# A linear-attention block gated with a SwiGLU block: the last 96 rows of w2 as 32-row matmuls, one row group per token tile

## The chip, the cores and the metric

The kernel runs on one core of one Trainium2 chip. The metric is the device time of one execution in microseconds. A core has TensorE (PE; its weight loads are listed apart as PEld), VectorE (DVE), ScalarE (ACT), GpSimd (POOL) and SyncE (SP), which here issues nearly all DMAs. The engines run their own instruction streams and wait for one another by semaphores.

## The reference, cut to what matters

```python
def _A_ref(x, wqkv, wo):                  # x: 1 x 2048 x 512, 32 heads of 16
    qkv = x @ wqkv                        # split in q, k, v
    phi = lambda t: jnp.where(t > 0, t + 1, jnp.exp(t)) + 1e-6
    pq, pk = phi(q), phi(k)
    kv = jnp.einsum("bhsd,bhse->bhde", pk, v)
    z = jnp.einsum("bhsd->bhd", pk)
    num = jnp.einsum("bhqd,bhde->bhqe", pq, kv)
    den = jnp.einsum("bhqd,bhd->bhq", pq, z)[..., None] + 1e-6
    return (num / den) @ wo               # heads put side by side again

def _B_ref(x, w1, w3, w2):                # F = 1376
    h = silu(x @ w1) * (x @ w3)           # 2048 x 1376
    return h @ w2                         # 2048 x 512

g = sigmoid((x * gate_w).sum(-1, keepdims=True))
return g * a + (1 - g) * b                # a = _A_ref(x, ..), b = _B_ref(x, ..)
```

All inputs and the output are bf16.

## The kernel before

The 2048 tokens are 16 tiles of 128 (NT), in 4 blocks of 512 (NTB blocks, TPB = 4 tiles each). F = 1376 is ten column groups of 128 (FC = 10) and a remainder of 96 (FR = 96), which starts at column F0 = 1280. A model dimension of 512 is four chunks of 128 (KC).

The order of work on each engine is the order in which the program issues it; nothing reorders it (the schedule is written out by hand). It has these stages.

First, for each token tile, the projections of q and k (line 169), their phi (lines 182 to 187), the running sum of pk over the tokens on POOL (line 201) and the accumulated product of pk and x (line 217). All weights and the transposed copies of x are loaded meanwhile, all on SP's queue; w2 comes last (lines 144 and 145). When the sum of pk is complete, SP transposes it (line 379), and a short chain of DVE work and two DMAs makes zb, the sum spread over all partitions.

Then come the four token blocks (line 463). In a block, `glu_step` runs for each of the ten column groups: four matmuls for the gate (line 264), four for the up projection (line 270), Silu on ACT (line 275) and the product on DVE (line 276), which writes the group's part of hT, the hidden layer with features on the partitions. In block 0 other work is set between the column groups: `kv_step` after group 2, `m2_step`, `z_order` and the first `den_products` after group 4, `den_step` after groups 5, 6, 8 and 9, and `rem_step(0)` after group 7.

`rem_step` computes the 96 remainder columns the other way round, with tokens on the partitions (16 matmuls of 193 columns, line 231: gate, up and the gating column), multiplies them on DVE into `hrem` (line 241), whose rows are padded with zeros to 128, and has a DMA transpose it into the eleventh chunk of hT (line 254).

`den_step(t)` makes the denominators of token tile t (DVE lines 287 to 294, POOL lines 283 and 298) and a DMA transposes the scaled tile into pqT (line 303).

After the column groups, `out_step` runs for each of the block's four token tiles. It sums a from pqT and M2 in four matmuls (line 429), which ACT scales by g into `aga` (line 434). Then it sums b in eleven matmuls (line 442): ten with 128 rows of hT and w2, the last one with the 96 remainder rows. DVE adds both (line 446), and SP stores the tile (line 459). Between the tiles of blocks 0 to 2 stand the `den_step` of the next block's tiles and, after tile 1, the `rem_step` of the next block. The last token tile of all is done in three column pieces.

PSUM has eight banks. `mm_tile` hands out banks 4 to 7 in turn, for column groups and remainder steps; `ab_tile` hands out banks 0 to 3 in turn, for the sums of a and b and for `kv_step` and `m2_step`. A matmul that takes a bank again waits until its last reader is done.

Of the kernel before, what the change touches and what calls it, by code (L numbers as in the profile page):

```python
# [9 lines left out]
ALU = mybir.AluOpType  # L10
AX = mybir.AxisListType
FP32 = mybir.dt.float32
BF16 = mybir.dt.bfloat16
# [3 lines left out]
def kernel(  # L17
# [17 lines left out]
    nc = tc.nc  # L35
    P = nc.NUM_PARTITIONS

    Bb, S, D = A_x.shape
    F = B_w1.shape[1]
# [5 lines left out]
    NTB = S // TB  # L45
    TPB = TB // P
    FC = F // P
    FR = F - FC * P
    F0 = FC * P
    HPC = P // Dh  # L50
    ZP = 4
    NR = 2 * FR + 1

    x2d = A_x.flatten_outer_dims()
    out2d = out.flatten_outer_dims()
# [5 lines left out]
    consts = ctx.enter_context(tc.tile_pool(name="consts", bufs=1))  # L61
# [13 lines left out]
        out=bmask[:], in_=bmask[:], pattern=[[-Dh, HPC], [0, Dh]], compare_op=ALU.is_ge,  # L75
# [3 lines left out]
        out=bmask[:], in_=bmask[:], pattern=[[Dh, HPC], [0, Dh]], compare_op=ALU.is_ge,  # L79
        fill=0.0, base=Dh - 1, channel_multiplier=-1,  # L80
    )
    hrem = [consts.tile([P, TPB, P], BF16, name=f"hrem{i}") for i in range(2)]
    for h in hrem:
        nc.gpsimd.memset(h[:], 0.0)
    zacc = consts.tile([P, D], FP32, name="zacc")
    zaccb = consts.tile([P, D], BF16, name="zaccb")
    zb = consts.tile([P, D], BF16, name="zb")
# [21 lines left out]
    dq = nc.sync  # L109
# [22 lines left out]
    with nc.allow_non_contiguous_dma(reason="gate column"):  # L132
        dq.dma_start(
            out=wr[:, :, 2 * FR : NR], in_=gate_w.rearrange("(kc d o) -> d kc o", d=P, o=1)
        )
# [7 lines left out]
    w2_r = B_w2[0:F0, :].rearrange("(fc f) d -> f fc d", f=P)  # L143
    dq.dma_start(out=w2[:, 0:FC, :], in_=w2_r)
    dq.dma_start(out=w2[:FR, FC, :], in_=B_w2[F0:F, :])

    pq = consts.tile([P, NT, D], BF16, name="pq")
    pqT = consts.tile([P, KC, S], BF16, name="pqT")
# [7 lines left out]
    bank = [psum.tile([P, D], FP32, name=f"bank{i}") for i in range(8)]  # L156
    turn = {"mm": 0, "ab": 0}

    def mm_tile():
        turn["mm"] += 1  # L160
        return bank[4 + (turn["mm"] - 1) % 4]

    def ab_tile():
        turn["ab"] += 1
        return bank[(turn["ab"] - 1) % 4]
# [56 lines left out]

    def rem_step(tb):

        hr = hrem[tb % 2]
        for half in range(2):
            ps = mm_tile()[:].rearrange("p (j n) -> p j n", j=2)
            for j in range(2):
                t = tb * TPB + half * 2 + j
                for kc in range(KC):  # L230
                    nc.tensor.matmul(  # L231
                        ps[:, j, 0:NR], lhsT=xT[:, kc, t * P : (t + 1) * P],
                        rhs=wr[:, kc, 0:NR], start=(kc == 0), stop=(kc == KC - 1),
                    )
            t0 = tb * TPB + half * 2
            sg = work.tile([P, 2, FR], BF16, tag="sgr", name="sgr")
            nc.scalar.activation(out=sg[:], in_=ps[:, :, 0:FR], func=ACT.Silu)
            nc.scalar.activation(
                out=th_all[:, t0 : t0 + 2], in_=ps[:, :, 2 * FR], func=ACT.Tanh, scale=0.5
            )  # L240
            nc.vector.tensor_tensor(
                out=hr[:, half * 2 : half * 2 + 2, 0:FR], in0=ps[:, :, FR : 2 * FR],
                in1=sg[:], op=ALU.mult,
            )
        tl = slice(tb * TPB, (tb + 1) * TPB)
        nc.vector.tensor_scalar(
            out=g_all[:, tl], in0=th_all[:, tl], scalar1=0.5, scalar2=0.5,
            op0=ALU.mult, op1=ALU.add,
        )
        nc.vector.tensor_scalar(  # L250
            out=omg_all[:, tl], in0=th_all[:, tl], scalar1=-0.5, scalar2=0.5,
            op0=ALU.mult, op1=ALU.add,
        )
        dq.dma_start(
            out=hT[tb][:, FC, :].rearrange("p (tt q) -> p tt q", q=P),
            in_=hr[:].rearrange("p tt f -> p (tt f)"), transpose=True,
        )

    def glu_step(tb, fc):
        fs = slice(fc * P, (fc + 1) * P)  # L260
        tok = slice(tb * TB, (tb + 1) * TB)
        g_ps = mm_tile()
        for kc in range(KC):
            nc.tensor.matmul(  # L264
                g_ps[:], lhsT=w1[:, kc, fs], rhs=xT[:, kc, tok],
                start=(kc == 0), stop=(kc == KC - 1),
            )
        u_ps = mm_tile()
        for kc in range(KC):
            nc.tensor.matmul(  # L270
                u_ps[:], lhsT=w3[:, kc, fs], rhs=xT[:, kc, tok],
                start=(kc == 0), stop=(kc == KC - 1),
            )
        sg = work.tile([P, TB], BF16, tag="sg", bufs=3, name="sg")
        nc.scalar.activation(out=sg[:], in_=g_ps[:], func=ACT.Silu)  # L275
        nc.vector.tensor_tensor(out=hT[tb][:, fc, :], in0=u_ps[:], in1=sg[:], op=ALU.mult)  # L276
# [28 lines left out]
    def den_step(t):  # L305

        den_sums(t)
        if t + 1 < NT:
            den_products(t + 1)
        den_scale(t)  # L310


    hT = {}
# [85 lines left out]
    def kv_step():  # L399
        kv_ps = ab_tile()[:].rearrange("p (c q) -> p c q", q=P)  # L400
        for c in range(KC):
            cs = slice(c * P, (c + 1) * P)
            for kc in range(KC):
                nc.tensor.matmul(  # L404
                    kv_ps[:, c, :], lhsT=wv[:, kc, cs], rhs=Gsb[:, kc, cs],
                    start=(kc == 0), stop=(kc == KC - 1),
                )
        nc.vector.tensor_tensor(
            out=kvT[:], in0=kv_ps,
            in1=bmask[:].rearrange("p h d -> p (h d)")[:, None, :].to_broadcast([P, KC, P]),  # L410
            op=ALU.mult,
        )

    def m2_step():
        for c in range(KC):
            ps = ab_tile()
            nc.tensor.matmul(ps[:], lhsT=kvT[:, c, :], rhs=wo[:, c, :], start=True, stop=True)  # L417
            if c % 2 == 0:
                nc.scalar.activation(out=M2[:, c, :], in_=ps[:], func=ACT.Copy)
            else:  # L420
                nc.vector.tensor_copy(out=M2[:, c, :], in_=ps[:])

    def out_step(tb, tt):
        t = tb * TPB + tt
        ts = slice(t * P, (t + 1) * P)
        tl = slice(tt * P, (tt + 1) * P)
        a_ps = ab_tile()
        for c in range(KC):
            nc.tensor.matmul(  # L429
                a_ps[:], lhsT=pqT[:, c, ts], rhs=M2[:, c, :],  # L430
                start=(c == 0), stop=(c == KC - 1),
            )
        aga = work.tile([P, D], FP32, tag="aga", name="aga")
        nc.scalar.activation(out=aga[:], in_=a_ps[:], func=ACT.Copy, scale=g_all[:, t : t + 1])  # L434
        o = work.tile([P, D], BF16, tag="o", bufs=3, name="o")
        last = t == NT - 1
        for lo, w in ((0, 2 * P), (2 * P, P), (3 * P, P)) if last else ((0, D),):
            cs = slice(lo, lo + w)
            b_ps = ab_tile()
            for fc in range(FC + 1):  # L440
                n = P if fc < FC else FR
                nc.tensor.matmul(  # L442
                    b_ps[:, 0:w], lhsT=hT[tb][:n, fc, tl], rhs=w2[:n, fc, cs],
                    start=(fc == 0), stop=(fc == FC),
                )
            nc.vector.scalar_tensor_tensor(  # L446
                out=o[:, cs], in0=b_ps[:, 0:w], scalar=omg_all[:, t : t + 1], in1=aga[:, cs],
                op0=ALU.mult, op1=ALU.add,
            )
            if t < 2:  # L450
                rows = out2d[0 : 2 * P, :].rearrange("(p j) d -> p j d", j=2)[:, t, :]
            else:
                rows = out2d[ts, :]
            if last and w == P:

                if lo + w < D:
                    continue
                cs = slice(2 * P, D)
            dq.dma_start(out=rows[:, cs], in_=o[:, cs])
# [3 lines left out]
    for tb in range(NTB):  # L463
        for fc in range(FC):
            glu_step(tb, fc)
            if tb == 0:
                if fc in den_at:
                    den_step(den_at[fc])
                if fc == 2:
                    kv_step()  # L470
                if fc == 4:
                    m2_step()
                    z_order()
                    den_products(0)
                if fc == 7:
                    rem_step(0)
        for tt in range(TPB):
            out_step(tb, tt)
            if tb + 1 < NTB:
                if tt == 0:  # L480
                    hT[tb + 1] = work.tile([P, FC + 1, TB], BF16, tag="hT", name="hT")
                if tt == 1:
                    rem_step(tb + 1)
                den_step((tb + 1) * TPB + tt)
# [30 lines left out]
```

## Time and profile before

| what | value |
|---|---|
| median of 3 runs | 179.36 us (178.71 to 179.49) |
| span of the profiled execution | 177.9 us, 2504 instructions |
| time of the profiled execution outside the span | the profile gives none; the median lies 1.46 us above the span |
| granted TensorE clock | 1.000 |
| PE busy | 174.3 us (98%), 879 instructions |
| PEld busy | 84.1 us (47%) |
| DVE busy | 101.5 us (57%) |
| ACT busy | 62.2 us (35%) |
| POOL busy | 63.5 us (36%) |
| DMA | 15.41 MB, mean 87 GB/s |

The span runs from the first to the last instruction of one execution; the time of a run is longer than that. Busy is the time in which an engine had an instruction under way. Matmuls overlap one another in the records, so 40 matmuls of 379 ns each need not take 40 x 379 ns; the spacing of their starts says what they cost. PEld, the weight loads, lie beside the matmuls.

### The profile page before, as it was taken

Reading aid. Unit: us, or ns where it says so; the run is one execution under the profiler, and the core shown is the slowest. Engines: PE = TensorE matmul, PEld = TensorE weight load, DVE = VectorE, ACT = ScalarE, POOL = GpSimd, SP = SyncE. Lnnn points to the kernel's source line nnn. Section 1 sums busy time; section 2 is a strip of 40 time slices with the busy share of each in tenths; the row PEclk is TensorE's granted clock in tenths of the full one; section 3 lists DMA queues with packets and bytes.
Section 4 is the critical chain, followed back from the end, with each engine's and each line's share of the span. In section 5 each row is a group of like instructions: output and inputs, shape, how many; then the busy total and the mean of one; then the engine's idle time right before and its main releaser. Section 6 shows DMA issues by size and latency. Waiting matters only on the chain.

```text
span 177.9 us, 2504 instructions
## 1 busy us (share of the span) xinstructions
PE 174.3 (98%) x879; PEld 84.1 (47%) x879; DVE 101.5 (57%) x195; ACT 62.2 (35%) x113; POOL 63.5 (36%) x105
## 2 busy tenths in 40 slices
PE   8999999999999999999999999999999999999993
PEld 5444444444454464644444464444445444444453
DVE  0299798888865888666344166634325564333222
ACT  3255444544744332331333223242321223342130
POOL 5077667557301676846300044540004432000000
DMA  6978959993103025243100013520000342000001
GB/s 175 266 209 233 168 100 315 391 350 111 33 0 29 0 55 66 66 95 106 29 0 4 0 33 85 94 57 4 0 0 29 88 92 59 0 0 0 29 33 59
DMA packets 29724, 15.41 MB, mean 87 GB/s; under 512 B 21552, under 2 KB 28048, under 8 KB 29712
## 3 DMA queue, kind: packets, MB, share of 16 engines
q1 hardware_dynamic: 29440, 15.25, 35.2%
q8 instruction: 7, 0.11, 0.3%
q10 hardware_dynamic: 272, 0.01, 0.1%
q14 instruction: 5, 0.04, 0.1%
HBM read 8.56 MB, written 2.10 MB: 60 GB/s over the span
## 4 chain that ended last, share of the span: by engine, by line
PE 98%; DVE 0%; issue 0%
PE bank L442 21%; PE bank L264 19%; PE bank L270 19%; PE bank L169 16%; PE bank L429 8%; PE bank L217 8%; PE bank L231 3%; PE bank L317 2%; PE bank L323 1%; PE bank L404 1%; PE bank L417 0%; DVE o L446 0%
## 5 line engine op out<-in xcount | busy, mean ns | idle before, releaser
L276 DVE TENSOR_TENSOR hT<-bank,sg 128x512 bf16<-128x512 f32 x40 | 27.3, 682 | 32.4 <-PE bank L270 32.4
L264 PE MATMUL bank<-xT,w 128*128 128x512 bf16 x160 | 41.1, 379 | 0.0
L270 PE MATMUL bank<-xT,w 128*128 128x512 bf16 x160 | 41.1, 379 | 0.0
L442 PE MATMUL bank<-w,hT 128*128 128x512 bf16 (+3 forms) x198 | 40.7, 355 | 0.0
L275 ACT ACTIVATE sg<-bank 128x512 bf16<-128x512 f32 x40 | 23.9, 597 | 46.7 <-PE bank L264 46.7
L298 POOL TENSOR_TENSOR pqs<-pq,rden 128x512 bf16<-128x512 bf16 x16 | 16.9, 1056 | 55.7 <-issue 48.2
L169 PE MATMUL bank<-wqk,xT 128*128 128x512 bf16 x128 | 31.2, 386 | 0.0
L442 PEld LDWEIGHTS <-hT 128*128 128x128 bf16 (+1 forms) x198 | 18.5, 98 | 19.8
L446 DVE SCALAR_TENSOR_TENSOR o<-bank,omg_all,aga 128x512 bf16<-128x512 f32 (+2 forms) x18 | 12.4, 692 | 25.6 <-PE bank L442 25.5
L201 POOL TENSOR_TENSOR zacc<-zacc,pk 128x128 f32<-128x128 f32 x56 | 23.3, 446 | 10.4 <-DVE pk L187 10.4
L270 PEld LDWEIGHTS <-w 128*128 128x128 bf16 x160 | 15.7, 98 | 18.9
L264 PEld LDWEIGHTS <-w 128*128 128x128 bf16 x160 | 15.6, 98 | 18.4
L434 ACT ACTIVATE aga<-bank,g_all 128x512 f32<-128x512 f32 x16 | 11.0, 688 | 28.9 <-PE bank L429 28.9
L169 PEld LDWEIGHTS <-xT 128*128 128x128 bf16 x128 | 12.6, 99 | 15.1 <-issue 0.6
L283 POOL TENSOR_TENSOR pr<-pq,zb 128x512 f32<-128x512 bf16 x16 | 18.5, 1156 | 0.1
L217 PE MATMUL bank<-pk,xN 128*128 128x512 bf16 x64 | 16.4, 379 | 0.0
L429 PE MATMUL bank<-M,pqT 128*128 128x512 bf16 x64 | 16.4, 378 | 0.0
L182 ACT ACTIVATE eq<-bank 128x512 bf16<-128x512 f32 x16 | 9.4, 598 | 16.0 <-PE bank L169 16.0
L187 DVE SCALAR_TENSOR_TENSOR pk<-bank,emk 128x512 bf16<-128x512 f32 x16 | 11.1, 692 | 1.6
L182 ACT ACTIVATE ek<-bank 128x512 bf16<-128x512 f32 x16 | 9.5, 597 | 7.1 <-PE bank L169 7.1
L187 DVE SCALAR_TENSOR_TENSOR pq<-bank,emq 128x512 bf16<-128x512 f32 x16 | 11.1, 692 | 0.5
L287 DVE TENSOR_REDUCE den<-pr 128x32 f32<-128x512 f32 x16 | 10.8, 676 | 0.0
(48 smaller groups left out, 82.6 us busy)
## 6 DMA issues: line engine op xcount, KB each, us to landing
w<-in_B_w_dram SPq DMA_DIRECT2D x3, 1280.0 KB, 10.1
out_dram<-o SPq DMA_DIRECT2D x15, 128.0 KB, 1.9
wqk<-in_A_wqkv_dram SPq DMA_DIRECT2D x4, 256.0 KB, 3.9
xN<-in_A_x_dram SPq DMA_DIRECT2D x1, 1024.0 KB, 5.8
xN<-in_A_x_dram SPq DMA_DIRECT2D x2, 256.0 KB, 3.1
xN<-in_A_x_dram SPq DMA_DIRECT2D x1, 512.0 KB, 3.7
wv<-in_A_wqkv_dram SPq DMA_DIRECT2D x1, 512.0 KB, 11.0
wo<-in_A_wo_dram SPq DMA_DIRECT2D x1, 512.0 KB, 12.0
```

The costliest lines, as they stand in the source:

```text
L169: nc.tensor.matmul(ps[:], lhsT=xT[:, kc, t * P : (t + 1) * P], rhs=w[:, kc, :], start=(kc == 0), stop=(kc == KC - 1),)
L182: nc.scalar.activation(out=e[:], in_=ps[:], func=ACT.Exp)
L187: nc.vector.scalar_tensor_tensor(out=dst, in0=ps[:], scalar=0.0, in1=em[:], op0=ALU.max, op1=ALU.add)
L201: nc.gpsimd.tensor_tensor(out=(zaccb if t == NT - 1 else zacc)[:, cs], in0=zacc[:, cs], in1=pk[t][:, cs], op=ALU.add,)
L217: nc.tensor.matmul(bank[kc][:], lhsT=xN[:, t, kc * P : (kc + 1) * P], rhs=pk[t][:], start=(t == 0), stop=(t == NT - 1),)
L264: nc.tensor.matmul(g_ps[:], lhsT=w1[:, kc, fs], rhs=xT[:, kc, tok], start=(kc == 0), stop=(kc == KC - 1),)
L270: nc.tensor.matmul(u_ps[:], lhsT=w3[:, kc, fs], rhs=xT[:, kc, tok], start=(kc == 0), stop=(kc == KC - 1),)
L275: nc.scalar.activation(out=sg[:], in_=g_ps[:], func=ACT.Silu)
L276: nc.vector.tensor_tensor(out=hT[tb][:, fc, :], in0=u_ps[:], in1=sg[:], op=ALU.mult)
L283: nc.gpsimd.tensor_tensor(out=pr[t][:], in0=pq[:, t, :], in1=zb[:], op=ALU.mult)
L429: nc.tensor.matmul(a_ps[:], lhsT=pqT[:, c, ts], rhs=M2[:, c, :], start=(c == 0), stop=(c == KC - 1),)
L442: nc.tensor.matmul(b_ps[:, 0:w], lhsT=hT[tb][:n, fc, tl], rhs=w2[:n, fc, cs], start=(fc == 0), stop=(fc == FC),)
```

## The change

For blocks 0 to 2 the 96 remainder rows of w2 are no longer the eleventh matmul of each token tile's sum. They are split into three sets of 32 rows (RG = 3, RP = 32). `rem_step` writes its products into `hrow` in an order in which, after one DMA transpose into `hrT`, partitions 32j to 32j + 31 of its piece r hold the features of set r for token tile j of the block. `w2x` holds the matching rows of w2 four times, once in each set of 32 partitions; four more DMAs load it behind w2. The new `rem_out_step` runs ahead of the block's `out_step`s: for each r it issues four 32-row matmuls, one for each token tile, which lie in four different row groups of the array and write four different banks. These begin the four sums of b, so banks 0 to 3 are held, one for each token tile, until the tile's ten 128-row matmuls have been added. The sums of a in these blocks take their banks from `mm_tile`. Block 3 keeps the form of before, with a single `hrem`. In block 0, `rem_step(0)` moves from after column group 7 to after column group 5.

```diff
--- before.py
+++ after.py
@@ -50,6 +50,8 @@
     HPC = P // Dh
     ZP = 4
     NR = 2 * FR + 1
+    RP = 32
+    RG = FR // RP
 
     x2d = A_x.flatten_outer_dims()
     out2d = out.flatten_outer_dims()
@@ -79,9 +81,11 @@
         out=bmask[:], in_=bmask[:], pattern=[[Dh, HPC], [0, Dh]], compare_op=ALU.is_ge,
         fill=0.0, base=Dh - 1, channel_multiplier=-1,
     )
-    hrem = [consts.tile([P, TPB, P], BF16, name=f"hrem{i}") for i in range(2)]
-    for h in hrem:
-        nc.gpsimd.memset(h[:], 0.0)
+    hrem = consts.tile([P, TPB, P], BF16, name="hrem")
+    nc.gpsimd.memset(hrem[:], 0.0)
+    hrow = [consts.tile([P, RG, TPB, RP], BF16, name=f"hrow{i}") for i in range(2)]
+    hrT = [consts.tile([P, RG, P], BF16, name=f"hrT{i}") for i in range(2)]
+    w2x = consts.tile([P, RG, D], BF16, name="w2x")
     zacc = consts.tile([P, D], FP32, name="zacc")
     zaccb = consts.tile([P, D], BF16, name="zaccb")
     zb = consts.tile([P, D], BF16, name="zb")
@@ -143,6 +147,9 @@
     w2_r = B_w2[0:F0, :].rearrange("(fc f) d -> f fc d", f=P)
     dq.dma_start(out=w2[:, 0:FC, :], in_=w2_r)
     dq.dma_start(out=w2[:FR, FC, :], in_=B_w2[F0:F, :])
+    w2x_r = B_w2[F0:F, :].rearrange("(r i) d -> i r d", i=RP)
+    for j in range(TPB):
+        dq.dma_start(out=w2x[j * RP : (j + 1) * RP, :, :], in_=w2x_r)
 
     pq = consts.tile([P, NT, D], BF16, name="pq")
     pqT = consts.tile([P, KC, S], BF16, name="pqT")
@@ -222,7 +229,7 @@
 
     def rem_step(tb):
 
-        hr = hrem[tb % 2]
+        tiled = tb + 1 < NTB
         for half in range(2):
             ps = mm_tile()[:].rearrange("p (j n) -> p j n", j=2)
             for j in range(2):
@@ -238,10 +245,18 @@
             nc.scalar.activation(
                 out=th_all[:, t0 : t0 + 2], in_=ps[:, :, 2 * FR], func=ACT.Tanh, scale=0.5
             )
-            nc.vector.tensor_tensor(
-                out=hr[:, half * 2 : half * 2 + 2, 0:FR], in0=ps[:, :, FR : 2 * FR],
-                in1=sg[:], op=ALU.mult,
-            )
+            up = ps[:, :, FR : 2 * FR]
+            if tiled:
+                for j in range(2):
+                    nc.vector.tensor_tensor(
+                        out=hrow[tb % 2][:, :, half * 2 + j, :],
+                        in0=up[:, j, :].rearrange("p (r i) -> p r i", i=RP),
+                        in1=sg[:, j, :].rearrange("p (r i) -> p r i", i=RP), op=ALU.mult,
+                    )
+            else:
+                nc.vector.tensor_tensor(
+                    out=hrem[:, half * 2 : half * 2 + 2, 0:FR], in0=up, in1=sg[:], op=ALU.mult,
+                )
         tl = slice(tb * TPB, (tb + 1) * TPB)
         nc.vector.tensor_scalar(
             out=g_all[:, tl], in0=th_all[:, tl], scalar1=0.5, scalar2=0.5,
@@ -251,10 +266,26 @@
             out=omg_all[:, tl], in0=th_all[:, tl], scalar1=-0.5, scalar2=0.5,
             op0=ALU.mult, op1=ALU.add,
         )
-        dq.dma_start(
-            out=hT[tb][:, FC, :].rearrange("p (tt q) -> p tt q", q=P),
-            in_=hr[:].rearrange("p tt f -> p (tt f)"), transpose=True,
-        )
+        if tiled:
+            dq.dma_start(
+                out=hrT[tb % 2][:], in_=hrow[tb % 2][:].rearrange("p r j i -> p (r j i)"),
+                transpose=True,
+            )
+        else:
+            dq.dma_start(
+                out=hT[tb][:, FC, :].rearrange("p (tt q) -> p tt q", q=P),
+                in_=hrem[:].rearrange("p tt f -> p (tt f)"), transpose=True,
+            )
+
+    def rem_out_step(tb):
+
+        for r in range(RG):
+            for j in range(TPB):
+                rows = slice(j * RP, (j + 1) * RP)
+                nc.tensor.matmul(
+                    bank[j][:], lhsT=hrT[tb % 2][rows, r, :], rhs=w2x[rows, r, :],
+                    start=(r == 0), stop=False,
+                )
 
     def glu_step(tb, fc):
         fs = slice(fc * P, (fc + 1) * P)
@@ -424,7 +455,8 @@
         t = tb * TPB + tt
         ts = slice(t * P, (t + 1) * P)
         tl = slice(tt * P, (tt + 1) * P)
-        a_ps = ab_tile()
+        tiled = tb + 1 < NTB
+        a_ps = mm_tile() if tiled else ab_tile()
         for c in range(KC):
             nc.tensor.matmul(
                 a_ps[:], lhsT=pqT[:, c, ts], rhs=M2[:, c, :],
@@ -436,12 +468,13 @@
         last = t == NT - 1
         for lo, w in ((0, 2 * P), (2 * P, P), (3 * P, P)) if last else ((0, D),):
             cs = slice(lo, lo + w)
-            b_ps = ab_tile()
-            for fc in range(FC + 1):
+            b_ps = bank[tt] if tiled else ab_tile()
+            nfc = FC if tiled else FC + 1
+            for fc in range(nfc):
                 n = P if fc < FC else FR
                 nc.tensor.matmul(
                     b_ps[:, 0:w], lhsT=hT[tb][:n, fc, tl], rhs=w2[:n, fc, cs],
-                    start=(fc == 0), stop=(fc == FC),
+                    start=(fc == 0 and not tiled), stop=(fc + 1 == nfc),
                 )
             nc.vector.scalar_tensor_tensor(
                 out=o[:, cs], in0=b_ps[:, 0:w], scalar=omg_all[:, t : t + 1], in1=aga[:, cs],
@@ -472,8 +505,10 @@
                     m2_step()
                     z_order()
                     den_products(0)
-                if fc == 7:
+                if fc == 5:
                     rem_step(0)
+        if tb + 1 < NTB:
+            rem_out_step(tb)
         for tt in range(TPB):
             out_step(tb, tt)
             if tb + 1 < NTB:
```

## The prediction

> **What bounds the kernel now.** I read the page's chain of the work that ended last first, then the groups of TensorE by form, then the same chain in order of time around the end of one token block, then the timeline of block 0 and the waits of the DMA-issuing SP.
>
> The chain by engine and line:
>
> ```profile
> PE 98%; DVE 0%; issue 0%
> PE bank L442 21%; PE bank L264 19%; PE bank L270 19%; PE bank L169 16%; PE bank L429 8%; PE bank L217 8%; PE bank L231 3%; PE bank L317 2%; PE bank L323 1%; PE bank L404 1%; PE bank L417 0%; DVE o L446 0%
> ```
>
> Nothing but TensorE sets the end, so a change is worth what it adds to or takes from TensorE's stream, and the waits that it puts into it. TensorE's waits have a single row, 0.8 us at the very start; there is no stall to recover.
>
> The forms of line 442, which the change touches (columns: line, engine, operation, out<-in, shapes, count | busy us, mean ns | idle before):
>
> ```profile
> L442 PE MATMUL bank<-w,hT 128*128 128x512 bf16 x150 | 34.8, 379 | 0.0
> L442 PE MATMUL bank<-w,hT 96*128 96x512 bf16 x15 | 5.7, 381 | 0.0
> L442 PEld LDWEIGHTS <-hT 96*128 96x128 bf16 x18 | 1.8, 98 | 1.8
> ```
>
> A 96-row matmul lasts as long as a 128-row one, so the last quarter of the array is paid for and unused. The 379 ns run from start to finish; the spacing comes from the chain in time (start, length, count):
>
> ```profile
> 68.27 2.38 PE bank L442 x11
> 70.64 0.87 PE bank L429 x4
> 71.51 2.38 PE bank L442 x11
> 73.89 1.34 PE bank L231 x16
> ```
>
> Eleven matmuls in 2.38 us are 216 ns each, the 96-row one among them; a matmul thus still runs 379 - 216 = 163 ns after the next has started. The weight loads (98 ns) lie wholly under the matmuls.
>
> The timeline where block 0 passes to its output, cut to what the steps below use:
>
> ```profile
> 52.06 1.06 PE L404 MATMUL bank<-Gsb,wv 128*128 128x128 bf16 x16
> ...
> 52.96 1.03 PE L264 MATMUL bank<-xT,w 128*128 128x512 bf16 x4
> ...
> 59.00 1.03 PE L264 MATMUL bank<-xT,w 128*128 128x512 bf16 x4
> 59.27 0.69 DVE L276 TENSOR_TENSOR hT<-bank,sg 128x512 bf16<-128x512 f32 x1 [0.70 <-PE bank L270]
> ...
> 62.32 3.86 SPq L303 DMA_TRANSPOSE pqT<-pqs  x2
> ...
> 64.29 0.61 DVE L241 TENSOR_TENSOR hrem<-bank,sgr 128x192 bf16<-128x192 f32 x2
> ...
> 66.27 1.22 SPq L254 DMA_TRANSPOSE hT<-hrem  x1
> ...
> 67.24 1.03 PE L429 MATMUL bank<-M,pqT 128*128 128x512 bf16 x4
> ```
>
> Line 404 is the useful neighbour: 16 matmuls with 16 different weight loads go by in 52.96 - 52.06 = 0.90 us, so a load-and-matmul pair can start every 56 ns. And SP:
>
> ```profile
> SPq L379 <- POOL zaccb L201: 9.8, 1, 9.8
> ```
>
> SP stands idle for 9.8 us between the last weight load and the transpose of zaccb.
>
> **TensorE, the part that decides.** Per block the change removes four 96-row matmuls: 4 x 216 = 864 ns. It adds twelve 32-row matmuls with twelve weight loads. No 32-row matmul stands in this trace, so the price is bounded.
>
> If four row groups stream side by side with no stagger, three rounds cost 3 x 216 = 648 ns, 216 ns less than before. If the pairs start 56 ns apart as at line 404, round follows round (4 x 56 = 224 ns, a hair over one matmul's 216), and the next full-height matmul must wait for the last group: 11 x 56 + 216 = 832 ns, 32 ns less than before. If the groups do not run side by side, twelve cost 12 x 216 = 2592 ns, 1728 ns more. I take 832, since line 404 is the nearest row with a new weight load for every short stretch of streaming.
>
> Twice per block the array also changes between full height and four groups. The trace has no such change. The lower bound is nothing: 128-row and 96-row matmuls follow each other at 216 ns today. The upper bound is that the array empties (163 ns, the overhang above) and the next weights are loaded only then (98 ns): 261 ns. I take the 163 ns, because loads run ahead everywhere in this trace: 326 ns per block.
>
> Per block: -864 + 832 + 326 = +294 ns; over three blocks +0.88 us. With bounds on both terms, groups side by side: from 3 x (648 - 864) = -0.65 us to 3 x (832 - 864 + 522) = +1.47 us.
>
> By the Trainium skill, "TensorEngine Tiling (Array Packing)", Key Properties, changing the tiling mode, not just the tile, drains TensorE; it gives no time, and no row here can show it. This is the rule that speaks against the change, and with the overhang as its price the sum is the +0.88 us above; without it, -0.1 us. By the skill's "TensorE: Matmul & The Clock Gate", Part 3, tiles of different row groups start about 4 ns apart, and four 32-row matmuls of 512 columns measured 3.07 times as fast as in sequence; with that stagger a round is 216 + 12 = 228 ns and the three blocks gain 3 x (864 - 684) = 0.54 us if the switches are free.
>
> **The rest, all beside the stream.**
>
> DVE: two 128x192 products per block (0.61 us, 305 ns each) become four 128x96. From 305 ns and the 682 ns of a 128x512 one, 1.18 ns per column and 78 ns fixed: 191 ns each, 766 against 610, +0.16 us per block. DVE waits for TensorE before 32 of the 40 products of line 276, 32.4 us in all or 1.0 us each, which covers it; uncovered it would be 0.5 us in all.
>
> rem_step(0) goes from after column group 7 to after 5. TensorE would run it from 59.00 to 60.34. DVE then does den_sums(0) (to 61.16), four products (61.93) and two small ones (62.26); the product of group 6 becomes ready at 59.27 + 1.34 + 1.73 = 62.34, so it is not late. Group 7 reuses the first remainder bank at about 62.07, freed at 61.55: 0.5 us in hand. On SP the remainder's transpose now stands ahead of pqT's tiles 1 to 3 and behind tile 0 (issued 62.32, 1.22 us): issued at 63.5, and with the page's 2.4 us to landing there at 65.9. The row-group matmuls want it at 67.24, 1.3 us later. At its old place it would land at 66.27 + 2.4 = 68.7, 1.4 us late. What is pushed back on SP is at most one issue, and pqT's tile 1, issued at about 65.2 to land at 67.6, is wanted only near 71.
>
> The transposes themselves shrink from four 128-column blocks to three. The four w2x loads (96 KB each, 0.39 MB, 1.1 us at the 350 GB/s of slice 9 of the page) go on SP between line 145 (its issue ends at 37.0) and line 379 (46.88): the 9.8 us idle covers them. Uncovered, zaccb's transpose would wait, and the z chain behind it has about 2.5 us (64.7 to 67.2) before pqT is wanted.
>
> Banks: a's four tiles move to the banks of the column groups; each reuses one given back by a product or Silu two tiles earlier. b's banks were read a whole block of column groups before, so holding them early waits for nobody. One memset fewer at the start is off the chain. All of this at nothing.
>
> **The sum.** The profiled span is 177.9 us; the page gives no time for that execution beyond its span, and the median of the shown runs is 179.36, 1.46 us more, which I leave as it is. 177.9 + 0.88 = 178.8 of span, 180.2 us by the median.
>
> **Rivals.**
>
> Free switches, the other side: groups stream together and loads stay ahead, as they do at 216 ns for 96 rows next to 128. Then only the rounds count: -0.1 to -0.65 us, 178.7 to 179.3, about 179.0. Against it: nothing in the trace shows a change of array layout. It decides when a switch costs under 16 ns at 56 ns spacing, or under 108 ns without stagger. The 4 ns rule above lands here, at 178.8.
>
> No overlap of groups: the change doesn't do what it says. 3 x 1.73 = +5.2 us, 184.5; with switches at 163 ns 185.5. For it: every matmul here costs 216 ns whatever its rows. Against: the groups share neither rows nor output banks.
>
> Loads set the pace: each group's load shows its whole 98 ns, 11 x 98 + 216 = 1294 ns, plus 326 for the switches, +0.76 us per block: +2.3 us, 181.6. Against it: line 404 at 56 ns. A late hrT in block 0, should SP run over 1.3 us behind, costs up to the 1.4 us of the old place and ends between 180.2 and 181.6 too.
>
> **Chances.** Groups side by side with switches paid (0 to +1.6 us): 0.43. Free switches: 0.28. Slow loads or a late transpose: 0.13. No overlap: 0.16. A difference of 0.5% (0.9 us) is about what a measurement of this kernel can tell from no change. The most that the sum allows is a gain of 0.65 us, so faster by over 0.5% needs runs that fall luckily on top of the free case: 0.08. My own case straddles the bound at +0.88: half of it, with slow loads and no overlap, makes slower by over 0.5%: 0.50. Within 0.5%: 0.42. The likeliest case's own range is 179.3 to 180.9. The range over cases runs from 178.6, the free case's end, to 182.0, past the slow loads, and leaves out no overlap.
>
> **What would show it.** In the changed profile the twelve 32-row matmuls of a block should take about 0.83 us from first start to last start plus 0.22, with starts 56 ns apart; a gap of about 160 ns should stand before the first of them and before the first matmul of line 429 behind them. No gap means free switches; starts 216 ns apart mean no overlap, starts 98 ns apart slow loads. A wait of TensorE on hrT in block 0 would break the SP step; a wait on a DVE row at line 276 the bank step. Any TensorE time changed outside these stretches would make the prediction wrong.

## The result and the profile after

The changed kernel took 179.63 us (median of 20 runs, 179.33 to 180.08), the kernel before 179.31 us beside it (20 runs, 178.58 to 179.80). The ratio is 1.0023, 95% interval 1.0012 to 1.0034: slower by 0.3 us, about a third of the 0.88 us that was forecast. Part of the spread is the clock: the five of the changed kernel's 20 runs with a granted clock of 0.997 or 0.998 took 179.87 to 180.08 us, the fifteen at 1.000 took 179.33 to 179.90. The profiled span of the changed kernel is 178.0 us, of the kernel before 177.9.

The chain that ended last, by engine and line, of the changed kernel:

```profile
PE 97%; issue 1%; ACT 0%; DVE 0%; ACTq 0%
PE bank L475 20%; PE bank L295 20%; PE bank L301 19%; PE bank L176 16%; PE bank L461 8%; PE bank L224 8%; PE bank L238 3%; PE bank L348 2%; PE bank L285 1%; PE bank L435 1%; PE bank L448 0%; PE bank L354 0%; ACT sg L306 0%; DVE o L479 0%; ACTq L306 0%
```

The lines are renumbered (264 is now 295, 270 is 301, 429 is 461, 442 is 475) and the row-group matmuls are line 285. TensorE still sets the end. Of the 903 matmul records 17 are missing from this trace; in the second profile of the same kernel (e9 below), which has all 903, "issue" is 0%.

The new group by its tile hrT (count: duration min/median/max in ns, first and last start in us):

```profile
L285 PEld LDWEIGHTS <-hrT x36: 90/93/94, 67.2 to 130.5; 32*128 32x128 bf16 x36
L285 PE MATMUL bank<-w2x,hrT x36: 374/374/385, 67.2 to 130.7; 32*128 32x512 bf16 x36
```

And TensorE's timeline of the changed kernel at the end of block 0 (start, us, instruction, count):

```profile
66.20 1.03 PE L301 MATMUL bank<-xT,w 128*128 128x512 bf16 x4
67.17 0.82 PE L285 MATMUL bank<-w2x,hrT 32*128 32x512 bf16 x12
67.92 1.04 PE L461 MATMUL bank<-M,pqT 128*128 128x512 bf16 x4
```

Twelve matmuls of 374 ns lie within 0.82 us, so they run side by side. Read record by record, the four of a round start within 10 ns of one another (67.165, 67.168, 67.171, 67.175) and the next rounds begin at 67.391 and 67.607. Two gaps frame them. The last full-height matmul starts at 66.853 and the first row-group one 312 ns later, 96 more than the usual 216. The last row-group matmul starts at 67.616 and the next full-height one 307 ns later, 91 more. The first weight load of the new kind does not run ahead either: it starts at 67.160, 5 ns before its matmul, where loads otherwise start some 200 ns before theirs.

The section on the kernel before says that nothing reorders the work of an engine. For weight loads the records show otherwise: the four loads of the second round start at 67.175 to 67.185, ahead of that round's first matmul at 67.391, although each belongs to its own matmul call. They go into the row groups in which the first round's matmuls have only just begun.

To see where the time of a run goes, I cut each execution in three: up to the first matmul of kv_step, from there to the last matmul's start, and from there to the end of the span. The middle piece as a window of the profile (start and end, length, then the busy time of PE, PEld, DVE, ACT and POOL), before and after:

```profile
52.06:174.91 122.85, 122.85 (x642) 60.22 (x641) 62.91 (x122) 37.33 (x71) 35.40 (x33) 1.00 0.18 39
```

```profile
51.89:174.69 122.80, 122.02 (x653) 59.50 (x665) 62.51 (x128) 37.33 (x71) 35.36 (x33) 1.00 0.16 38
```

Everything that the change does to TensorE's stream, with its rounds, switches, banks and the moved step, makes this piece 0.05 us shorter. (PE's 122.02 after is no idle time: 12 of the missing records lie here, 653 matmuls against 665 loads.) The end is another matter. From the last matmul's start to the end of the span it is 3.02 us before and 3.27 after. The program ends with SP waiting for the DMA semaphores, the counters by which a DMA reports that it has landed; the waits on the last store (us in total, times, longest), before and after:

```profile
SPq L510 <- DMA out_dram<-o: 0.9, 1, 0.9
```

```profile
SPq L545 <- DMA out_dram<-o: 1.2, 1, 1.2
```

The last store itself lands 1.53 us after its issue before and 1.54 after. The DMAs take eight semaphores in turn. With 72 DMAs the last store falls on the last of them, with 76 on the fourth. SP then checks the eight in five instructions, one every 62 to 69 ns; the last store's stands in the fifth of these before and in the first after, so four more checks (0.26 us) come behind the landing instead of ahead of it. Before, the first check ran at 175.9 us with the store still under way; after, at 176.9, once it had landed (first and last start stand behind the durations):

```profile
L510 SPq EVENT_SEMAPHORE  x7: 17/28/28, 175.9 to 177.9; - x7
```

```profile
L545 SPq EVENT_SEMAPHORE  x7: 17/28/28, 176.9 to 177.9; - x7
```

So the rows give -0.05 + 0.26 = +0.21 us, which is theory T of the expectations below: a ratio of 1.0012 against the measured 1.0023 (1.0012 to 1.0034).

### The profile page after: what moved, and what is told of

It is laid out like the page before. It is cut to its first block, busy times and chain, and to the rows that moved or that the text cites. A ratio compares the mean times of both kernels' runs of the same rounds, so it can differ in the third digit from the quotient of the medians.

```text
span 178.0 us, 2542 instructions
## 1 busy us (share of the span) xinstructions
PE 173.1 (97%) x886; PEld 83.4 (47%) x903; DVE 101.1 (57%) x201; ACT 62.2 (35%) x113; POOL 63.0 (35%) x104
## 4 chain that ended last, share of the span: by engine, by line
PE 97%; issue 1%; ACT 0%; DVE 0%; ACTq 0%
PE bank L475 20%; PE bank L295 20%; PE bank L301 19%; PE bank L176 16%; PE bank L461 8%; PE bank L224 8%; PE bank L238 3%; PE bank L348 2%; PE bank L285 1%; PE bank L435 1%; PE bank L448 0%; PE bank L354 0%; ACT sg L306 0%; DVE o L479 0%; ACTq L306 0%
## 5 line engine op out<-in xcount | busy, mean ns | idle before, releaser
L295 PE MATMUL bank<-xT,w 128*128 128x512 bf16 x157 | 40.9, 379 | 0.3
L301 PE MATMUL bank<-xT,w 128*128 128x512 bf16 x156 | 40.4, 379 | 0.1
L475 PE MATMUL bank<-w,hT 128*128 128x512 bf16 (+4 forms) x182 | 37.7, 353 | 0.2
L475 PEld LDWEIGHTS <-hT 128*128 128x128 bf16 (+1 forms) x186 | 17.4, 98 | 18.4
```

Source lines behind the costliest of these rows:

```text
L295: nc.tensor.matmul(g_ps[:], lhsT=w1[:, kc, fs], rhs=xT[:, kc, tok], start=(kc == 0), stop=(kc == KC - 1),)
L301: nc.tensor.matmul(u_ps[:], lhsT=w3[:, kc, fs], rhs=xT[:, kc, tok], start=(kc == 0), stop=(kc == KC - 1),)
L475: nc.tensor.matmul(b_ps[:, 0:w], lhsT=hT[tb][:n, fc, tl], rhs=w2[:n, fc, cs], start=(fc == 0 and not tiled), stop=(fc + 1 == nfc),)
```

## The experiments

Of each profile the three pieces are given in one table at the end of this section. They are cut from the records of the trace.

**e1, full height.** As the changed kernel, but four 96-row matmuls at the head of the block's sums; hrem and its transpose as before the change.

```diff
-        for r in range(RG):
-            for j in range(TPB):
-                rows = slice(j * RP, (j + 1) * RP)
-                nc.tensor.matmul(
-                    bank[j][:], lhsT=hrT[tb % 2][rows, r, :], rhs=w2x[rows, r, :],
-                    start=(r == 0), stop=False,
-                )
+        for j in range(TPB):
+            nc.tensor.matmul(
+                bank[j][:], lhsT=hT[tb][:FR, FC, j * P : (j + 1) * P], rhs=w2[:FR, FC, :],
+                start=True, stop=False,
+            )
```

> The changed kernel with everything moved and held as it is there, but the remainder of a block done in four 96-row full-height matmuls at the head of the sums instead of twelve 32-row ones; the four w2x loads are issued and not read. Theory T (the rounds run at 3 x 216 ns and two switches of about 100 ns each eat the gain, so TensorE's stream is the same as before to 0.05 us; the time that is left over comes from the end of the program, where SP waits for its eight DMA semaphores one after the other and the last store's semaphore now stands four places earlier, 4 x 65 ns = 0.26 us): about 0.26 us over the kernel before, like the changed kernel; four matmuls take 864 ns from the first start to the next matmul's start, with no gap. Rival S (the row groups or the switches cost the 0.3 us in a way that the trace does not show): the kernel before to within 0.1 us.

Measured: 179.44 us against 179.46, ratio 0.9998 (0.9984 to 1.0012). The middle piece is 122.81 us, the end 3.27 us, both as in the changed kernel (122.80 and 3.27). By its rows T is right: rounds with switches cost what four full-height matmuls cost. The time of the runs leaves both theories standing, since T's 1.0012 is the interval's upper end and S's 1.0 lies in the middle.

**e2, the loads alone.** The kernel before with the four w2x loads and nothing that reads them.

```diff
     dq.dma_start(out=w2[:FR, FC, :], in_=B_w2[F0:F, :])
+    w2x_r = B_w2[F0:F, :].rearrange("(r i) d -> i r d", i=32)
+    for j in range(TPB):
+        dq.dma_start(out=w2x[j * 32 : (j + 1) * 32, :, :], in_=w2x_r)
```

> The kernel before with nothing but the four w2x loads added behind w2; nothing reads them. Theory T: 76 DMAs instead of 72, the last store falls on the fourth of the eight semaphores, so SP has four more waits after it has landed: +0.26 us over the kernel before, and after the last store's landing about 1.1 us to the end of the span where before shows 0.85. Rival S: no change. Rival L (the loads delay the z chain or other transfers that TensorE waits for): a wait of TensorE on a DMA or a DVE row in block 0.

Measured: 179.70 us against 179.46, ratio 1.0013 (0.9999 to 1.0027). The middle piece is that of the kernel before, 122.85 us; the end is 3.28 us. From the landing of the last store to the end of the span it is 1.11 us, against 0.85 before, as foretold, and SP's last wait grew:

```profile
SPq L514 <- DMA out_dram<-o: 1.2, 1, 1.2
```

Four loads that no instruction reads lengthen the end by 0.26 us and leave TensorE's stream alone: against L.

**e3, eight loads.** The changed kernel with each load cut in two.

```diff
-        dq.dma_start(out=w2x[j * RP : (j + 1) * RP, :, :], in_=w2x_r)
+        for lo, hi in ((0, 1), (1, RG)):
+            dq.dma_start(out=w2x[j * RP : (j + 1) * RP, lo:hi, :], in_=w2x_r[:, lo:hi, :])
```

> The changed kernel with each w2x load cut in two, so eight loads and 80 DMAs; same bytes. Theory T: the last store is back on the last of the eight semaphores, 0.26 us less than the changed kernel: between 0.1 us under and 0.1 us over the kernel before. Rival S: like the changed kernel, 0.3 us over the kernel before. Rival L: a little more than the changed kernel, since SP issues four DMAs more.

Measured: 179.23 us against 179.46, ratio 0.9990 (0.9976 to 1.0004). With four DMAs more than the changed kernel, the end is back at 3.00 us and SP's wait at the value of before:

```profile
SPq L546 <- DMA out_dram<-o: 0.9, 1, 0.9
```

The count of DMAs, not their work, sets the end.

**e4, rounds set apart.** In blocks 1 and 2 one round ahead of column group 8, one ahead of group 9, one in the old place.

```diff
+            if tb in (1, 2) and fc >= FC - 2:
+                rem_out_step(tb, [fc - (FC - 2)])
             glu_step(tb, fc)
...
-            rem_out_step(tb)
+            rem_out_step(tb, range(RG) if tb == 0 else [2])
```

> The changed kernel, with the three rounds of blocks 1 and 2 set apart: one ahead of column group 8, one ahead of group 9, one where all three were. Eight switches more in all. Theory T with a fixed price of about 100 ns for each switch: +0.8 us over the changed kernel, 1.1 over the kernel before, and the same 0.1 us gap ahead of and behind each round. If the 0.1 us belongs to the first use of hrT and not to the switch: no change against the changed kernel. With the 163 ns of the prediction for each switch: +1.3 us over the changed kernel.

Measured: 180.54 us against 179.46, ratio 1.0054 (1.0038 to 1.0071). The middle piece is 123.67 us, 0.87 more than in the changed kernel: 109 ns for each of the eight switches. TensorE's timeline in block 1:

```profile
94.44 1.03 PE L301 MATMUL bank<-xT,w 128*128 128x512 bf16 x4
95.40 0.39 PE L285 MATMUL bank<-w2x,hrT 32*128 32x512 bf16 x4
95.73 1.04 PE L295 MATMUL bank<-xT,w 128*128 128x512 bf16 x4
```

Four full-height matmuls take 0.86 us; the round stands 0.96 behind their start, and the next full-height matmul starts 0.33 behind the start of the round instead of 0.216. The price is one of the switch and is paid in both directions.

**e5, six rounds.** Each round issued twice.

```diff
-        for r in range(RG):
+        for n in range(2 * RG):
+            r = n % RG
...
-                    start=(r == 0), stop=False,
+                    start=(n == 0), stop=False,
```

> The changed kernel with the three rounds issued twice in each stretch, which adds the remainder twice to b; the number of switches stays. Theory T: a round is one matmul's 216 ns and no more, so 3 blocks x 3 rounds x 216 = +1.94 us over the changed kernel, with the gaps ahead of and behind the stretch as they are. If the 0.2 us of a block's gaps grow with the number of 32-row matmuls (weight loads that show): +2.5 us. With starts 56 ns apart as in the prediction: 12 x 56 = 672 ns a block, +2.0 us, to be told from T by the starts in the trace.

Measured: 181.19 us against 179.41, ratio 1.0104 (1.0080 to 1.0128). The middle piece is 124.75 us, 1.95 more than in the changed kernel: nine more rounds at 216 ns. The stretch of block 0 in TensorE's timeline:

```profile
67.07 1.47 PE L286 MATMUL bank<-w2x,hrT 32*128 32x512 bf16 x24
68.48 1.04 PE L462 MATMUL bank<-M,pqT 128*128 128x512 bf16 x4
```

It lasts 1.41 us to the next matmul, against 0.75 for three rounds. Within a round the starts stand 2 to 5 ns apart and not 56, and the twenty-four weight loads cost nothing beyond the rounds.

**e6, one load.** The kernel before with the first of the four loads only.

```diff
     dq.dma_start(out=w2[:FR, FC, :], in_=B_w2[F0:F, :])
+    w2x_r = B_w2[F0:F, :].rearrange("(r i) d -> i r d", i=32)
+    dq.dma_start(out=w2x[0:32, :, :], in_=w2x_r)
```

> The kernel before with one more load (96 KB into a tile that nothing reads), so 73 DMAs. Theory T: the last store falls on the first of the eight semaphores and SP has seven waits more after its landing, 7 x 65 ns = 0.46 us over the kernel before: a quarter of the added bytes of the four loads, and a larger loss than theirs. Rival L (bytes or DMA issues cost): a quarter of the four loads' loss, under 0.1 us. TensorE's stretch from the first matmul of kv_step to its last matmul stays at 122.85 us in both.

Measured: 179.41 us against 179.41, ratio of the runs 1.0011 (0.9997 to 1.0024). The middle piece is 122.85 us, as expected; the end is 3.11 us, 0.09 more than before, not 0.46. The count of seven waits was wrong: SP checks the eight semaphores in five instructions, three of them two DMA semaphores at once, and the first semaphore shares the third. So two checks come behind the landing, 59 and 121 ns after it, where the kernel before has one, 17 ns after it. The wait on the last store lies between the 0.9 of before and the 1.2 of four loads:

```profile
SPq L513 <- DMA out_dram<-o: 1.1, 1, 1.1
```

**e7, one row group.** All twelve matmuls of a block on partitions 0 to 31.

```diff
-                rows = slice(j * RP, (j + 1) * RP)
+                rows = slice(0, RP)
```

> The changed kernel with all twelve 32-row matmuls of a block on partitions 0 to 31, one row group, still into four banks; the remainder of token tiles 1 to 3 is then computed from tile 0's values. If the side-by-side running comes from the row groups: starts 216 ns apart, 9 x 216 = 1.94 us a block more, +5.8 us over the changed kernel. If four banks alone are what it takes: no change. The gaps ahead of and behind the stretch stay at about 0.1 us in both.

Measured: 185.56 us against 179.76, ratio 1.032 (1.029 to 1.035). The middle piece is 128.60 us, 5.80 more than in the changed kernel. TensorE's timeline:

```profile
67.20 2.76 PE L285 MATMUL bank<-w2x,hrT 32*128 32x512 bf16 x12
69.89 1.04 PE L461 MATMUL bank<-M,pqT 128*128 128x512 bf16 x4
```

Same shapes, same four banks, but starts 216 ns apart: four different row groups are what makes a round cost one matmul.

**e8, full height without the loads.** e1 without the four w2x loads.

```diff
-    w2x_r = B_w2[F0:F, :].rearrange("(r i) d -> i r d", i=RP)
-    for j in range(TPB):
-        dq.dma_start(out=w2x[j * RP : (j + 1) * RP, :, :], in_=w2x_r)
```

> The full-height variant (four 96-row matmuls at the head of a block's sums, b banks held, a in the other banks, rem_step(0) after group 5) without the w2x loads, so 72 DMAs and the last store on the last semaphore as before. Theory T: the stream as in the variant with the loads, 0.04 us under before, and the end as before: the kernel before to within 0.1 us, 0.2 to 0.25 us under the changed kernel. Rival S: if holding banks or moving rem_step(0) costs anything outside what the rows show, it stays at 0.2 to 0.3 us over the kernel before.

Measured: 179.13 us against 179.41, ratio 0.9994 (0.9980 to 1.0009). The middle piece is 122.81 us, the end 3.00. TensorE's timeline:

```profile
65.95 1.03 PE L279 MATMUL bank<-xT,w 128*128 128x512 bf16 x4
66.82 1.03 PE L263 MATMUL bank<-w,hT 96*128 96x512 bf16 x4
67.68 1.03 PE L439 MATMUL bank<-M,pqT 128*128 128x512 bf16 x4
```

The four 96-row matmuls take 0.86 us to the next start, with no gap on either side. Holding banks, moving a's sums and moving rem_step(0) cost nothing that the rows show.

**e9, the changed kernel once more**, on the chip of e6 and e8.

> The changed kernel itself, unchanged, to stand beside the two others of this call on the same chip. Theory T: TensorE's stretch from kv_step on 0.05 us shorter than before, the end 0.26 us longer, +0.2 us over the kernel before. Rival S (something of the change that the trace does not show): +0.3 us or more with the same rows.

Measured: 179.43 us against 179.41, ratio 1.0005 (0.9991 to 1.0018). The middle piece is 122.80 us, the end 3.28, as in its first profile.

**e10, rem_step(0) back.** The changed kernel with rem_step(0) after group 7.

```diff
-                if fc == 5:
+                if fc == 7:
                     rem_step(0)
```

> The changed kernel with rem_step(0) back behind column group 7. By the prediction's SP step the transpose of hrow lands about 1.4 us after TensorE wants hrT in block 0: a wait of TensorE on hrT of 1.2 to 1.5 us there, +1.2 to 1.5 us over the changed kernel. Rival: the landing is early enough or another wait hides it, no change.

Measured: 180.97 us against 179.76, ratio 1.0071 (1.0046 to 1.0097). The middle piece is 124.09 us, 1.28 more than in the changed kernel, and TensorE waits where it was said to:

```profile
PE bank L285 <- DMA hrT<-hrow: 1.2, 1, 1.2
```

The pieces, in us:

| kernel | DMAs | first matmul of kv_step | to the last matmul | to the end of the span |
|---|---|---|---|---|
| before | 72 | 52.06 | 122.85 | 3.02 |
| after | 76 | 51.89 | 122.80 | 3.27 |
| after again (e9) | 76 | 51.49 | 122.80 | 3.28 |
| e1 | 76 | 51.92 | 122.81 | 3.27 |
| e2 | 76 | 51.60 | 122.85 | 3.28 |
| e3 | 80 | 51.66 | 122.80 | 3.00 |
| e4 | 76 | 52.03 | 123.67 | 3.28 |
| e5 | 76 | 51.80 | 124.75 | 3.28 |
| e6 | 73 | 52.46 | 122.85 | 3.11 |
| e7 | 76 | 51.93 | 128.60 | 3.28 |
| e8 | 72 | 51.64 | 122.81 | 3.00 |
| e10 | 76 | 51.45 | 124.09 | 3.28 |

The middle repeats to 0.01 us among kernels with the same stream, and the end to 0.02 among those whose last store has the same semaphore. The first piece wanders over 1 us, between two profiles of the same kernel by 0.4. That is more than the effect under study, and enough to let the two comparisons of the changed kernel come out at 1.0023 and 1.0005, both with T's 1.0012 in or at the edge of their intervals. In the comparisons of e1, e2, e3, e6 and e8 too the value that the rows give lies in the interval or at its edge; but so does no change, in all but the very first. So the profiles show that the end moved, and the times of the runs agree with it without showing it by themselves. The nearest that they come is side by side on one chip: 179.13 us with 72 DMAs (e8) and 179.43 with 76 (e9), 179.23 with 80 (e3) and 179.44 and 179.70 with 76 (e1, e2); but the kernel before, also with 72, stands at 179.41 beside the first two and 179.46 beside the others. Whether the changed kernel also starts later by a tenth of a microsecond can't be told from one profile each; that stays open. Neither e3 (0.9990) nor e8 (0.9994) can be told from the kernel before; by their rows they gain about 0.05 us.

## Why the prediction was wrong, point by point

The bound was read rightly: TensorE's stream sets the end, no wait was added, and the stream changed only around the remainder's matmuls: the stretch of line 285 with its two gaps, and a few nanoseconds at each change of height that is no longer made.

The side was right by the runs (slower, by the interval), but by luck, for another cause. The stream, which was to lose 0.88 us, gained 0.05. The step that failed is the TensorE sum of a block, -864 + 832 + 326 = +294 ns. The twelve matmuls cost 667 ns and not 832, the two switches 197 and not 326, and the sum is 0. So two terms were mis-sized, both upwards.

The first is the stagger. Line 404 was taken as the price of a load-and-matmul pair, 56 ns, and the twelve were put at 832 ns. That row's matmuls are 128 columns long, and 56 ns is about a quarter of the 216 of a 512-column one: it shows a short matmul's own time, not what a weight load takes to pass. It was an upper bound read as a price. In the trace the loads of a round start 3 ns apart, and from the first row-group matmul to the next full-height one are 758 ns, of which 91 belong to the gap behind and 19 to the stagger and to a first round of 226 ns. The lower bound, 648, was the nearer one. The Trainium skill's "TensorE: Matmul & The Clock Gate", Part 3, puts the starts of tiles of different row groups about 4 ns apart; the trace agrees with its 3 ns.

The second is the switch, put at the 163 ns by which a matmul overhangs. It costs 96 ns on the way in, 91 and another 10 on the way out, and 109 each over the eight of e4. By the Trainium skill, "TensorEngine Tiling (Array Packing)", Key Properties, a change of tiling mode drains TensorE; the trace agrees in so far as each switch shows a gap. The end of a matmul in the records (379 ns) is no measure of that gap, since the first row-group matmul starts 312 ns after the last full-height one.

As recorded, the gap stands ahead of the weight load and is not the load's own 91 ns: the first load starts 307 ns after the last full-height matmul and its matmul 5 ns later, on the way out 303 and 4. In e10, where TensorE had waited for over a microsecond, the first row-group matmul also starts 4 ns after its load. What the load waits for at a switch stays open.

Together: three rounds 648, gaps 96 + 91 + 10, stagger and first round 19, which makes 864 ns, just what four 96-row matmuls took. e1 shows the same from the other side. The 0.05 us that the stream did gain is nearly all in e1 and e8 as well: in the trace of before, the first matmul behind a change between 128 and 96 rows is followed by the next after 218 to 220 ns instead of 216, on the way into a token tile's remainder and on the way out; grouped by block there are fewer such changes.

A step was also missing, the end of the program. The four w2x loads were costed at nothing because SP stood idle, and SP did issue them in that idle time (37.1 to 38.95, with the z chain untouched). But every DMA also moves on the turn of the eight semaphores, and I never asked which of them the last store would take: 0.26 us.

The rest held. The hrT transpose was issued at 63.43 (63.5 predicted), TensorE did not wait for it, and e10 shows 1.2 us of waiting at the old place against 1.4. DVE's four products last 248 ns each and not 191, but in the records they overlap: in block 1 a pair takes 0.42 us from its first start to its last end, where the one product of before took 0.36. That is 0.13 us more in a block, near the 0.16 of the prediction, and it stays covered. Of the rivals, no overlap, slow loads and a late transpose are out; free switches named the right round price but not the gaps.

## What to carry to other kernels

Running row groups side by side saves whole matmul slots, but each visit to that array layout cost about 0.2 us here, one 512-column slot: a stretch must save more than one slot to be worth having, and here it saved one. When a price is taken from a neighbouring row, ask what limited that row. Where a kernel differs by a few tenths of a microsecond, cut the trace into start, body and end before looking for a mechanism in the body: here the body was equal and the end had moved.

## What the runs showed that I had not expected

The number of DMAs in the program changes the length of its end by up to 0.26 us or a little more: with 72 or 80 DMAs the span ends 3.00 to 3.02 us after the last matmul's start, with 73 after 3.11 and with 76 after 3.27 or 3.28, with the last store's landing 1.53 to 1.54 us after its issue in all of them. Cutting each of four loads in two can thus make a kernel shorter (e3 against the changed kernel, by the end of the span).
